# Three tiny softmax steps on ScalarE in place of VectorE, and the softmax released two sums earlier

## The chip, the cores and the metric

The kernel runs on one core of a Trainium2 chip, in FP32 throughout. The metric is the device time of one execution in microseconds; the kernel before takes 706.02 us, the median of three executions (704.77 to 706.29). The engines are named as in the profile: PE (TensorE matmul), PEld (its weight loads), DVE (VectorE), ACT (ScalarE), POOL (GpSimd) and SP (SyncE, which issues the DMAs).

## The reference

Two stages follow each other. The first is a cross attention in both directions between 512 rows x and 32 state rows per head, for 8 batches and 8 heads of width 64. The second is a feed-forward layer with an ELU over all 4352 resulting rows (per batch 512 from x and 32 from the state).

```python
B, H, S, Ns, D = (8, 8, 512, 32, 64)
scores = scale * np.matmul(x, state.transpose(0, 1, 3, 2))
scores = scores - scores.max(-1, keepdims=True)
a = np.exp(scores)
a /= a.sum(-1, keepdims=True) + 1e-09
xread = np.matmul(a, state)
scores2 = scale * np.matmul(state, x.transpose(0, 1, 3, 2))
scores2 = scores2 - scores2.max(-1, keepdims=True)
a2 = np.exp(scores2)
a2 /= a2.sum(-1, keepdims=True) + 1e-09
sread = np.matmul(a2, x)
x = np.concatenate([xread, sread], axis=2)      # then (B,H,S,D) -> (B*S, H*D)
h = x @ w_in                                    # 512 -> 2048
g = np.where(h > 0.0, h, np.exp(np.minimum(h, 0.0)) - 1.0)
out = g @ w_out                                 # 2048 -> 512
```

There are two softmaxes per batch over the same products: one over the 32 states for each row of x, and one over the 512 rows for each state.

## The kernel before, in words

**The work of a batch.** The scores of a batch lie in two PSUM banks: the 32 states of eight heads are 256 rows, in two groups g of 128, and the 512 rows of x are their columns. `softmax` (from line 751) turns them by blocks of 32 with DVE transposes into `xr`, reduces over the states (128x16 per group), subtracts on POOL, exponentiates on ACT, sums on DVE, adds eps and inverts 32 totals per partition, multiplies on POOL, and transposes into `aT`, the attention weights over the states. `softmax_rows` (from line 737) works on the same scores as they lie, over the 512 columns of each state: a maximum per row on DVE, a 128x2 step that multiplies both maxima by -scale, two exponentials on ACT that add up the totals, a 128x2 step that adds eps, and a reciprocal. The scale, eps and maxima are in the buffer `small`, 68 columns wide; batches 0 and 1 have theirs in `sec`.

The attention output is not formed for the rows of x. The weights w_in are first multiplied with the state (`make_m`, in the profile the matmuls ps<-w_half,kT), and the first phase of the FFN multiplies the result `m` with `aT` (`ffn1_chunk`, four chunks, matmuls ps<-aT,m; ELU on ACT and DVE into `g`). The second phase (`ffn2`) multiplies `g` with w_out in 128x128 passes, eight matmuls to a product. Both phases, and the split of each half, use sums of operands in a seven-product scheme in place of eight products: DVE and POOL form sums such as `s`, `sec`, `g` and sums of `aT` and `m`, PE does seven products of them, and DVE or ACT gather each product from its PSUM bank into `o` (the row o<-o,ps, called an eviction here). A product can't start before its operand sums are made, and its bank is free only after the eviction of the product that had it.

For the state rows, `move_state` turns the row weights on DVE (two transposes into `xr`) and moves them between partitions with 16 DMAs of 32 KB on SP (xr<-xr); `state_read` multiplies them with x (matmuls ps<-xe,xr), and ACT scales the result with the reciprocal totals into `kT` (ps,small). The rows of all batches go through the FFN at the end (`states`).

**The stages.** `start` and `ffn2_1` are a prologue of batches 0 and 1, in which ACT and DVE also convert the weights from memory into what the products need. Then `batch(b)` runs for b = 2 to 7, each with the first phase of batch b and `ffn2`, in which the scores, `make_m`, the softmax and the state's move of batch b+1 are also written. So the softmax of the next batch runs on DVE, ACT and POOL beside the second phase of the present one. This is called a transition here. `sum_a` and `sum_m`, written behind the softmax, are POOL's sums of `aT` and `m`.

**What sets the order.** Nothing is issued as it is written. Each operation is recorded with a cost, its operands and a `port` flag (in class `Engine`, from line 464; nearly all rows of the profile therefore carry L464), and the class `Plan` makes a list schedule of them (line 1587, `plan.order(3, 40.0)`): PE takes the ready operation that was written first, POOL keeps the written order, and DVE, ACT and SP take the ready operation whose due time is nearest, due times being counted back from PE's order. The planner lets only one operation with the flag `port` run on DVE or POOL at a time. The engines then carry out their lists in order. `plan.behind(op)` makes what is recorded within depend on op. In `ffn2` the list `late` collects such points: late[4] is the last of the sums for product 6 (`second[6].sums`), late[5] a sum o.a12 - o.s, late[6] the last of the sums for product 7 (`second[7].sums`). In `soft_next` (line 1320) the next batch's softmax, its rows, the load of x, the state's move and POOL's sums are recorded behind late[6].

Of the kernel before, what the change touches and what calls it, by code (L numbers as in the profile page):

```python
# [16 lines left out]
AF = mybir.ActivationFunctionType  # L17
ALU = mybir.AluOpType
# [16 lines left out]
def elements(ap):  # L35
    n = 1
    for k in ap.shape[1:]:
        n *= k
    return n
# [350 lines left out]
def kernel(  # L390
# [21 lines left out]
    scale = 1.0 / math.sqrt(D)  # L412
    eps = 1e-9
# [16 lines left out]
    plan = Plan(psum)  # L430
# [28 lines left out]
    def issue(engine, name, kw):  # L459
        def emit():  # L460
            named = {k: resolve(v) for k, v in kw.items()}
            if name == "memset":
                named["ap"] = named.pop("out")
            ins = getattr(engine, name)(**named)  # L464
            tc.keep_in_program_order(ins)

        return emit

    def is_ap(v):
        return isinstance(v, (View, bass.AP))  # L470

    class Engine:
# [3 lines left out]
        def __getattr__(self, name):  # L476
            def call(**kw):
                outs = [kw[k] for k in ("out", "accum_out") if k in kw]
                ins = [v for k, v in kw.items() if k not in ("out", "accum_out") and is_ap(v)]
                n = max(elements(a) for a in outs + ins) / 1000  # L480
                wide = [a for a in ins if not isinstance(a, View) and elements(a) > 4]
                port = False
                if self.key == DVE:
                    cost = 0.07 + 1.042 * n
                    alone = len(wide) == 1 and not isinstance(kw["out"], View)
                    if alone and name in ("tensor_scalar", "tensor_copy"):
                        cost, port = 0.07 + 0.53 * n, True
                    port = port or len(wide) > 1
                elif self.key == ACT:
                    cost = 0.055 + 0.84 * n  # L490
                    cost += 0.1 * sum(k in kw and is_ap(kw[k]) for k in ("scale", "bias") if k in kw)
                    cost += 0.1 * ("accum_out" in kw)
                else:
                    cost = 0.06 + (1.86 if name == "tensor_tensor" and n > 0.3 else 2.45) * n
                    port = True
                plan.add(
                    self.key, cost, issue(self.engine, name, kw), ins, outs, port,
                    name=name,
                )

            return call

    V, A, Q = Engine(DVE, nc.vector), Engine(ACT, nc.scalar), Engine(POOL, nc.gpsimd)
# [56 lines left out]
    def bc(ap, n):  # L560
        return ap[:, :, None].to_broadcast(list(ap.shape) + [n])
# [6 lines left out]
    def small(b):  # L568
        return small_2 if b > 1 else sec_1[:, 1152:1220]

    def tops(b, g):
        small_b = small(b)
        return dict(
            top=small_b[:, g : g + 1], total=small_b[:, 2 + g : 3 + g],
            top_t=small_b[:, 4 + 16 * g : 20 + 16 * g], total_t=small_b[:, 36 + 16 * g : 52 + 16 * g],
        )
# [150 lines left out]
    def soft_t(b, g):  # L727
        return (xr if b > 1 else soft)[:, g * 512 : (g + 1) * 512]

    def soft_a(b, g):  # L730
        at = xr if b > 1 else s_buf if b else sec_2
        return at[:, (b > 0) * 1024 + g * 512 :][:, :512]

    def read(b, late=False):
        return kT[:, (b - 1) % (B + 1)] if b != 1 or not late else read_1

    def softmax_rows(b):
        s = st[b, "s"]
        top, total = small(b)[:, 0:2], small(b)[:, 2:4]
        for g in range(G):  # L740
            V.reduce_max(out=tops(b, g)["top"], in_=s[g], axis=AX_X)
        V.tensor_scalar(out=top, in0=top, scalar1=-scale, scalar2=None, op0=ALU.mult)
        for g in range(G):
            A.activation(
                out=soft_a(b, g), in_=s[g], func=AF.Exp, scale=scale, bias=tops(b, g)["top"],
                accum_out=tops(b, g)["total"],
            )
        V.tensor_scalar(out=total, in0=total, scalar1=eps, scalar2=None, op0=ALU.add)
        V.reciprocal(out=total, in_=total)

    def softmax(b, to):
        s = st[b, "s"]
        total_t = small(b)[:, 36:68]

        def rows(g):
            return soft_t(b, g).rearrange("p (k n) -> p k n", n=NS)

        for g in range(G):
            V.transpose(out=soft_t(b, g), in_=s[g])
        for g in range(G):  # L760
            V.reduce_max(out=tops(b, g)["top_t"], in_=rows(g), axis=AX_X)
            (V if 0 & 1 and b > 1 or b in [] else Q).tensor_tensor(
                out=rows(g), in0=rows(g), in1=bc(tops(b, g)["top_t"], NS), op=ALU.subtract
            )
            A.activation(out=soft_t(b, g), in_=soft_t(b, g), func=AF.Exp, scale=scale)
            V.reduce_sum(out=tops(b, g)["total_t"], in_=rows(g), axis=AX_X)
        V.tensor_scalar(out=total_t, in0=total_t, scalar1=eps, scalar2=None, op0=ALU.add)
        V.reciprocal(out=total_t, in_=total_t)
        for g in range(G):
            (V if 0 & 2 and b > 1 or b in [] else Q).tensor_tensor(  # L770
                out=rows(g), in0=rows(g), in1=bc(tops(b, g)["total_t"], NS), op=ALU.mult
            )
            V.transpose(out=to[:, g * 512 : (g + 1) * 512], in_=soft_t(b, g))
# [502 lines left out]
    def ffn2(o, b):  # L1276

        c11, c12, c21, c22 = (o.part(i, j) for i in range(2) for j in range(2))
        nxt = b + 1 < B
        spare = spaces(m_sb[:, 1], 3)  # L1280
        o.sum_1()
        late = [plan.ops[-1]]
        if 0:
            second[1].sums(o.a11, spare + s_2[0][:1])
            steps = second[1].steps(c12, fresh=True)
            steps[0]()
        else:
            x1 = o.open()
            o.product(x1, o.a11, b11, True)
            A.copy(out=c12, in_=x1)  # L1290
            steps = []
        if nxt:
            first_m(b + 1, 1)
            scores(b + 1, xr, [f.view() for f in fixed])
        else:
            turn_read()
        for f in steps[1:]:
            f()
        second[2].sums(o.a12, s_2[1] + spaces(a_sb))
        late.append(plan.ops[-1])  # L1300
        for f in second[2].steps(c11, base=c12):
            f()
        late.append(plan.ops[-1])
        second[4].sums(o.a22, s_2[0] + spare[:2])
        late.append(plan.ops[-1])
        for f in second[4].steps(c21, fresh=True):
            f()
        second[6].sums(o.s, s_2[1] + spaces(a_sb))
        late.append(plan.ops[-1])
        combine(o.a12, o.a12, o.s)  # L1310
        late.append(plan.ops[-1])
        steps = second[6].steps(c12)
        second[7].sums(o.a21, s_2[0])
        late.append(plan.ops[-1])
        for f in steps:
            f()
        combine(o.s, o.s, o.a11, ALU.add)
        late.append(plan.ops[-1])

        def soft_next():  # L1320
            if nxt:
                with plan.behind(late[6]):
                    softmax(b + 1, a_sb)
                    softmax_rows(b + 1)
                    load_x(b + 1, x_halves)
                    move_state(b + 1)
                    sum_a()
                    if 1:
                        sum_m(m_to[0])
        if 1==1: soft_next()  # L1330
        V.tensor_tensor(out=c21, in0=c21, in1=c12, op=ALU.add)
        steps = second[7].steps(c22, fresh=True)
        second[5].sums(o.s, s_2[1])
        late.append(plan.ops[-1])
        if 1==2: soft_next()
        for f in steps:
            f()
        V.tensor_tensor(out=c21, in0=c21, in1=c22, op=ALU.add)
        steps = second[5].steps(c12)
        second[3].sums(o.a12, s_2[0])  # L1340
        for f in steps:
            f()
        V.tensor_tensor(out=c22, in0=c22, in1=c12, op=ALU.add)
        store(b, 1, o)
        steps = second[3].steps(c12)
        if nxt:
            make_m(b + 1, 2, 3)
            copy_m(b + 1, 1, m_to[1])
            sum_m(m_to[1])
            state_read(b + 1)  # L1350
        for f in steps:
            f()
        store(b, 0, o)
# [269 lines left out]
```

## Time and profile before

| | before |
|---|---|
| median of three executions | 706.02 us (704.77 to 706.29) |
| the profiled execution | 707.31 us |
| its span, first to last instruction | 705.5 us |
| TensorE clock granted | 0.997 |
| PE busy | 692.4 us, 98% |
| DVE busy | 577.5 us, 82% |
| ACT busy | 301.3 us, 43% |
| POOL busy | 139.4 us, 20% |
| tensor_scalar 128x2 in small on DVE, 12 | 7.5 us, mean 625 ns |
| tensor_scalar 128x32 in small on DVE, 6 | 1.0 us, mean 174 ns |
| tensor_scalar 128x2 in sec on DVE, 4 | 1.7 us, mean 431 ns |

The profile is of one execution, and its durations are compared with its own time. The 1.8 us between the profiled time and the span lie outside the instructions that it records. A line of a timeline gives start, length, engine, line of the kernel, operation, output<-inputs, shapes and how many instructions it stands for; in brackets follow the idle time before it and what ended that. In a line of groups the total busy time and the mean of one in ns stand after the bar, then the engine's idle time ahead of them. [...] Shares of busy time are averages over stages; the stages are seen in windows.

### The profile page before, as it was taken

Reading aid. Unit: us, or ns where it says so; the run is one execution under the profiler, and the core shown is the slowest. Engines: PE = TensorE matmul, PEld = TensorE weight load, DVE = VectorE, ACT = ScalarE, POOL = GpSimd, SP = SyncE. Lnnn points to the kernel's source line nnn. Section 1 sums busy time; section 2 is a strip of 40 time slices with the busy share of each in tenths; the row PEclk is TensorE's granted clock in tenths of the full one; section 3 lists DMA queues with packets and bytes.
Section 4 is the critical chain, followed back from the end, with each engine's and each line's share of the span. In section 5 each row is a group of like instructions: output and inputs, shape, how many; then the busy total and the mean of one; then the engine's idle time right before and its main releaser. Section 6 shows DMA issues by size and latency. Waiting matters only on the chain.

```text
span 705.5 us, 14564 instructions
## 1 busy us (share of the span) xinstructions
PE 692.4 (98%) x5802; PEld 591.9 (84%) x5802; DVE 577.5 (82%) x1015; ACT 301.3 (43%) x604; POOL 139.4 (20%) x161
## 2 busy tenths in 40 slices
PE   8899999999999999999999999999999999999997
PEld 7544468889988998889888988899888988899996
DVE  3989999999659895899769995989589976997650
ACT  3999982011157123831275125712383127600530
POOL 1310000042121045101630153103520173000000
PEclk9999999999999999999999999999999999999999
DMA  8677773203261406650283316440575026200300
GB/s 193 208 275 256 265 240 58 60 33 118 91 141 70 120 2 181 149 121 1 60 245 77 70 44 189 98 121 1 153 177 120 2 59 212 62 1 31 120 8 23
DMA packets 111268, 78.55 MB, mean 111 GB/s; under 512 B 89184, under 2 KB 92768, under 8 KB 111200
## 3 DMA queue, kind: packets, MB, share of 16 engines
q1 hardware_dynamic: 108988, 77.06, 38.6%
q8 instruction: 46, 0.75, 0.4%
q10 hardware_dynamic: 2212, 0.56, 0.4%
q14 instruction: 22, 0.18, 0.1%
HBM read 61.34 MB, written 13.11 MB: 106 GB/s over the span
## 4 chain that ended last, share of the span: by engine, by line
PE 82%; DVE 12%; DMA 2%; issue 2%; ACT 1%; SPq 1%; ACTq 0%; DVEq 0%
PE ps L464 82%; DVE small L464 3%; DVE o L464 3%; DVE sec L464 2%; DVE s L464 2%; DMA xe<-in_x_dram 1%; DVE g L464 1%; DMA g<-in_x_dram 1%; SPq L464 1%; DVE xr L464 0%; DVE aT L464 0%; PE ps L1581 0%; ACT sec L464 0%; ACT t_w L464 0%; ACTq L464 0%
## 5 line engine op out<-in xcount | busy, mean ns | idle before, releaser
L464 PE MATMUL ps<-aT,m 128*128 128x256 f32 (+1 forms) x568 | 148.8, 406 | 1.1 <-ACT kT L464 1.1
L464 PE MATMUL ps<-w_out,g 128*128 128x128 f32 (+1 forms) x864 | 144.5, 315 | 0.0
L464 PEld LDWEIGHTS ps<-w_out,g 128*128 128x128 f32 x864 | 126.6, 191 | 14.7 <-issue 6.2
L464 PEld LDWEIGHTS ps<-aT,m 128*128 128x128 f32 x568 | 105.1, 190 | 29.1 <-issue 13.1
L464 DVE TENSOR_TENSOR o<-o,ps 128x128 f32<-128x128 f32 (+2 forms) x239 | 66.6, 282 | 50.0 <-PE ps L464 48.5
L464 ACT COPY o<-ps 128x128 f32<-128x128 f32 (+2 forms) x70 | 23.2, 335 | 153.5 <-PE ps L464 153.5
L464 POOL TENSOR_TENSOR xr<-xr,small 128x512 f32<-128x512 f32 x24 | 26.9, 1140 | 306.9 <-PE ps L464 156.9
L464 POOL TENSOR_TENSOR m<-m 128x256 f32<-128x256 f32 x72 | 65.9, 937 | 70.8 <-ACT m L464 69.4
L464 PE MATMUL ps<-sec 128*128 128x128 f32 x560 | 74.0, 275 | 0.0
L464 PEld LDWEIGHTS ps<-sec 128*128 128x128 f32 x560 | 68.4, 192 | 0.4
L464 PE MATMUL ps<-t_w,s 128*128 128x128 f32 (+1 forms) x432 | 65.1, 300 | 3.1 <-DVE o L464 3.1
L464 PEld LDWEIGHTS ps<-t_w,s 128*128 128x128 f32 x432 | 58.4, 191 | 7.3 <-DVE o L464 4.1
L464 ACT ACTIVATE xe<-ps 128x512 f32<-128x512 f32 x96 | 55.5, 600 | 19.5 <-DVE ps L464 12.8
L464 ACT COPY m<-ps 128x512 f32<-128x512 f32 (+1 forms) x56 | 27.1, 535 | 71.8 <-PE ps L464 71.7
L464 ACT COPY sec<-ps 128x512 f32<-128x512 f32 (+1 forms) x52 | 29.8, 574 | 46.0 <-PE ps L464 45.9
L464 DVE SCALAR_TENSOR_TENSOR g<-xe,ps 128x512 f32<-128x512 f32 x66 | 43.7, 679 | 1.2 <-ACT xe L464 1.2
L464 DVE TENSOR_SCALAR xe<-xe 128x512 f32<-128x512 f32 x30 | 15.7, 527 | 31.2 <-ACT xe L464 26.1
L464 PE MATMUL ps<-aT,s 128*128 128x256 f32 x168 | 40.9, 382 | 0.0
L464 ACT ACTIVATE xe<-xe 128x512 f32<-128x512 f32 x66 | 40.0, 637 | 0.9
L464 DVE TENSOR_TENSOR ps<-sec,ps 128x512 f32<-128x512 f32 (+1 forms) x52 | 34.8, 669 | 5.7 <-PE ps L464 4.2
L464 PEld LDWEIGHTS ps<-aT,s 128*128 128x128 f32 x168 | 31.3, 190 | 6.4 <-issue 2.1
L464 PE MATMUL ps<-w_half,kT 64*32 64x256 f32 x1024 | 35.0, 382 | 0.0
(152 smaller groups left out, 1157.4 us busy)
## 6 DMA issues: line engine op xcount, KB each, us to landing
w_half<-w_in_mem SPq DMA_DIRECT2D x54, 512.0 KB
t_w<-in_moe_w_out_dram SPq DMA_DIRECT2D x8, 1024.0 KB
t_w<-in_moe_w_in_dram SPq DMA_DIRECT2D x7, 1024.0 KB
out_dram<-o SPq DMA_DIRECT2D x14, 512.0 KB
xe<-in_x_dram SPq DMA_DIRECT2D x26, 256.0 KB
o<-in_x_dram SPq DMA_DIRECT2D x80, 64.0 KB
w_in_mem<-w_half SPq DMA_DIRECT2D x8, 512.0 KB
xr<-xr SPq DMA_DIRECT2D x96, 32.0 KB
```

The lines of the kernel that those rows point to most:

```text
L464: ins = getattr(engine, name)(**named)
```

## The change

A helper `line` does a tiny step as an ACT activation Copy with an immediate scale and bias, in place of a DVE tensor_scalar with one constant. It serves three steps: the maxima times -scale (128x2), the row totals plus eps (128x2) and the state totals plus eps (128x32). Its condition b >= 0 holds for all eight batches. In the planner's costs, every tensor_scalar of DVE gets the `port` flag, also one on few elements. In `soft_next` the softmax and what is recorded with it stand behind late[4] instead of late[6].

```diff
                     if alone and name in ("tensor_scalar", "tensor_copy"):
-                        cost, port = 0.07 + 0.53 * n, True
+                        cost = 0.07 + 0.53 * n
+                    port = name == "tensor_scalar" or alone and name == "tensor_copy"
                     port = port or len(wide) > 1
...
+    def line(b, x, a, c):
+        if b >= 0:
+            A.activation(out=x, in_=x, func=AF.Copy, scale=a, bias=c)
+        elif c:
+            V.tensor_scalar(out=x, in0=x, scalar1=c, scalar2=None, op0=ALU.add)
+        else:
+            V.tensor_scalar(out=x, in0=x, scalar1=a, scalar2=None, op0=ALU.mult)
+
     def softmax_rows(b):
...
-        V.tensor_scalar(out=top, in0=top, scalar1=-scale, scalar2=None, op0=ALU.mult)
+        line(b, top, -scale, 0.0)
...
-        V.tensor_scalar(out=total, in0=total, scalar1=eps, scalar2=None, op0=ALU.add)
+        line(b, total, 1.0, eps)
...
-        V.tensor_scalar(out=total_t, in0=total_t, scalar1=eps, scalar2=None, op0=ALU.add)
+        line(b, total_t, 1.0, eps)
...
         def soft_next():
             if nxt:
-                with plan.behind(late[6]):
+                with plan.behind(late[4]):
                     softmax(b + 1, a_sb)
```

## The prediction

> **What bounds the kernel now.** I read the page's busy shares first, then windows of 10 us, the waits, and the timelines of PE, DVE and POOL in one transition.
>
> ```profile
> PE 692.4 (98%) x5802; PEld 591.9 (84%) x5802; DVE 577.5 (82%) x1015; ACT 301.3 (43%) x604; POOL 139.4 (20%) x161
> 40.00:50.00 10.00, 10.00 (x86) 4.38 (x85) 9.90 (x14) 9.40 (x19) 0.00 (x0) 1.00 0.68 232
> 330.00:340.00 10.00, 9.20 (x80) 8.82 (x79) 10.00 (x21) 2.13 (x7) 3.88 (x5) 1.00 0.01 2
> ```
>
> PE is busy 98% of the span. In the second line (columns after the length: PE, PEld, DVE, ACT, POOL) PE is full, but DVE and ACT are nearly full as well: the prologue, where batches 0 and 1 run beside the weight conversion. In the third PE misses 0.80 us while DVE is full and ACT has time. Five windows have such a hole, one per transition of batches 2 to 7; between 40 and 700 us PE is otherwise full. So only holes in PE, or work added to PE, move the time.
>
> The timeline of PE in that window, then of DVE, then of POOL:
>
> ```profile
> 334.43 1.06 PE L464 MATMUL ps<-t_w,s 128*128 128x128 f32 x8
> 335.32 1.06 PE L464 MATMUL ps<-sec 128*128 128x128 f32 x8
> 337.00 1.16 PE L464 MATMUL ps<-t_w,s 128*128 128x128 f32 x8 [0.62 <-DVE o L464]
> 338.00 1.06 PE L464 MATMUL ps<-sec 128*128 128x128 f32 x8
> 339.24 1.16 PE L464 MATMUL ps<-sec,s 128*128 128x128 f32 x8 [0.18 <-DVE o L464]
> ```
>
> ```profile
> 333.12 0.17 DVE L464 TENSOR_SCALAR small<-small 128x32 f32<-128x32 f32 x1
> 334.21 1.01 DVE L464 TENSOR_SCALAR small<-small 128x2 f32<-128x2 f32 x1
> 335.33 1.42 DVE L464 TENSOR_TENSOR sec<-g 128x512 f32<-128x512 f32 x1
> 336.67 0.28 DVE L464 TENSOR_TENSOR o<-o,ps 128x128 f32<-128x128 f32 x1
> 337.50 0.24 DVE L464 TENSOR_TENSOR o<-o,ps 128x128 f32<-128x128 f32 x1
> 337.67 0.72 DVE L464 TENSOR_SCALAR small<-small 128x2 f32<-128x2 f32 x1
> ```
>
> ```profile
> 333.89 2.31 POOL L464 TENSOR_TENSOR xr<-xr,small 128x512 f32<-128x512 f32 x2 [7.69 <-DVE small L464]
> 337.65 0.72 POOL L464 TENSOR_TENSOR aT<-aT 128x256 f32<-128x256 f32 x1 [1.45 <-DVE aT L464]
> ```
>
> Groups of eight matmuls start 0.89 us apart (335.32 - 334.43). From 335.32 to 337.00 it is 1.68: PE lost 0.79, because the eviction that frees its PSUM bank (336.67, which ends at 336.95) was queued on DVE behind the 1.42 us sum and the 1.01 us tiny step. 338.00 to 339.24 is 0.35 too long, behind the 0.72 us tiny step. The first loss is in all five transitions (0.78 each), the second in two (0.345): 5 x 0.78 + 2 x 0.345 = 4.6 us, all that a change in the steady state can win by filling holes. The view of waits says much the same, less the start-up after each hole, and shows where the softmax idles:
>
> ```profile
> PE ps L464 <- DVE o L464: 3.7, 8, 0.6
> ...
> ACT xr L464 <- POOL xr L464: 21.6, 11, 3.7
> ACT xr L464 <- DVE small L464: 19.0, 6, 3.8
> ```
>
> [...] the 2-column step at 334.21 lasts 1.01 us inside POOL's 333.89 to 336.20, and the 32-column one ahead of it 0.17. [...] the trace holds a single table load of 1.28 us, so I cost table switches at nothing.
>
> ```profile
> L464 DVE TENSOR_SCALAR small<-small 128x2 f32<-128x2 f32 x12 | 7.5, 625 | 0.0
> L464 ACT ACTIVATION_READ_ACCUMULATOR xr<-ps,small 128x1 f32 x12 | 2.4, 196 | 0.0
> L464 ACT ACTIVATE kT<-ps,small 128x64 f32<-128x64 f32 x12 | 3.2, 329 | 0.0
> ```
>
> **The change, part by part.** (1) 24 tiny steps leave DVE for ACT: three per softmax, eight softmaxes. In a transition DVE is relieved of 0.17 + 1.01 + 0.72 = 1.9 us. Not all is a gain: part of it was waiting for POOL, and the next two-input sum inherits the wait. ACT gains 3 x 0.2 = 0.6 us where it is busy 2.13 of 10; that alone costs nothing.
>
> (2) The softmax may start after the sums of product 6, no longer after product 7's. In the new written order its reduces stand about 6 us earlier on DVE (I follow the order with the pitches of the old trace: evictions 0.20, sums of 512 0.60, transposes 0.63, reduces 0.60). In the transition shown the row reduces then end near 322, ACT's scale near 322.2, exp rows near 323.8, the eps steps at 324.2 and 327.3, the reciprocals at 328.3. POOL multiplies from 328.4 to 331.6, the transposes into aT follow at 330.8 to 332.8, and POOL's sums of aT run from 332 to 340. The old places were 333.89 and 337.65. What is late next: these POOL steps now meet DVE's two-input sums for products 5 and 3 (s 128x1024, sec and s 128x512). By that reckoning the operand s of a t_w,s product, read at PE's 338.33, is ready at 338.49 (about 0.16 us of stall); three other places have 0.2 to 0.4 of slack. I take 0.25 per transition, with bounds of 0 and 0.8: 5 x 0.25 = 1.25 stays of the 4.6.
>
> (3) The changed port flag alters nothing by itself: with the old flag the written order of the changed kernel comes out the same, since the only steps it would mark anew are now on ACT. But new costs and an earlier softmax make the planner order everything anew. On PE the scores of the moved state (the xe,xr run) now stand between runs of full passes in all six transitions, where they used to adjoin the kT run. In the old trace the starts at the borders of such an isolated run are 93 and 101 ns too far apart, 0.2 us together: 6 x 0.2 = +1.2 us (bounds 0 and 1.5). Nothing hides that: PE is full.
>
> (4) The state's move is 16 DMAs on SP, about 0.63 us from issue to issue, each landing about 1.9 us later. The first now goes at about 334.5, so the last starts near 344 and lands near 346, with the load of the next w_half beside them; the xe,xr run starts near 347.6. Slack 1.2 us: no cost. If the first were over 1.2 us later, PE would lose the excess in each transition.
>
> (5) In the prologue six of the steps join an ACT that is 9.40 to 10.00 of 10 busy: 6 x 0.2 = 1.2 us more ACT time, and as much less on DVE (431 ns each there). Queued behind them are ACT's evictions and exponentials, for which PE waits with slack of 0.06 to 1.1 us near 48 and 65 us. PE enters its full stretch about 0.16 us later in the new order; I take +0.5 (bounds -0.5 and +1.5).
>
> Sum: -4.6 + 1.25 + 1.2 + 0 + 0.5 = -1.65 us. The profiled execution took 707.31 (span 705.5), so it would take 705.7 (span 703.9). The median shown, 706.02, is 1.3 lower; the same difference gives **704.4**. About 0.2%, 1.4 us, is what a measurement of this kernel can tell from no change: faster is below 704.6, slower above 707.4.
>
> **Rivals.** *All of it comes* (0.24): no stall left, the prologue neutral: -4.6 + 1.2 = -3.4, 702.6. For: the hole hangs on tiny steps that vanish from DVE. Against: POOL keeps as much work and DVE as many two-input sums[...].
>
> *The stall only moves* (0.18): [...] PE stalls 0.78 per transition at another place: -4.6 + 3.9 + 1.2 + 0.5 = +1.0, 707.0. For: the new order has four two-input sums inside 332 to 340. Against: those have 0.2 us of slack where the eviction in the old order had less than none.
>
> *Slower by the prologue* (0.12): ACT works in written order. A tiny step that waits for a DVE reduce blocks the exponentials behind it; with six of them and DVE itself 9.90 of 10 busy, a wait of 0.7 us each, about one reduce, is 4.2 us that both engines lack, and PE follows. With the steady state's -4.6 + 1.25 + 1.2 that is +2.05, and with the switching of ACT to late work about +2.5: 708.5. It decides from 3.5 us of prologue loss up (-4.6 + 1.25 + 1.2 + 3.5 = +1.35). For: the windows above. Against: only two softmaxes are there.
>
> **How the numbers follow.** The likeliest case has 0.46 (its own range 703.2 to 705.6, from the bounds of 3 and 5 in part); it gives 0.265 faster, 0.17 same, 0.025 slower. The full gain gives 0.24 faster. The moved stall splits 0.01, 0.08, 0.09, the prologue 0, 0.02, 0.10. Sums: faster 0.52, same 0.27, slower 0.21. The range 702.2 to 707.6 leaves out about a third of the full gain at its low end, and most of the prologue case.
>
> **What would show it.** Right: no TENSOR_SCALAR of 2 columns in `small` on DVE, twelve ACTIVATE of about 0.2 us on ACT; in the windows of the five transitions PE over 9.6; the wait of PE for DVE o below 1.5 us in all. Step 2: POOL's xr,small steps within 1 us after its reciprocal, near 5 us earlier relative to the transition. Step 3: the isolated xe,xr run with 0.1 us at each border. Step 4 wrong: PE waits for a DMA xr<-xr. Step 5: the start of batch 2's first phase compared in both traces; more than 1.5 us late means the prologue rival. The prediction fails if PE's holes stay at 0.8 under another name, or if the new order opens holes that the old did not have.

## The result, and the profile after

The changed kernel takes 703.02 us, the median of 20 executions (702.0 to 706.83), against 705.94 us of 20 executions of the kernel before. The ratio is 0.9966, 95% interval 0.9958 to 0.9975: faster by 0.34%, 1.8 to 3.0 us. The forecast was 704.4. The profiled execution took 704.65 us with a span of 702.9 (before 707.31 and 705.5).

First the busy shares and the windows of the transition that the prediction followed (columns after the length: PE, PEld, DVE, ACT, POOL):

```profile
PE 692.8 (99%) x5794; PEld 591.0 (84%) x5794; DVE 563.8 (80%) x991; ACT 303.9 (43%) x628; POOL 144.2 (21%) x161
320.00:330.00 10.00, 10.00 (x92) 10.00 (x92) 9.79 (x23) 3.44 (x11) 3.12 (x4) 1.00 0.00 0
330.00:340.00 10.00, 10.00 (x113) 9.34 (x112) 8.37 (x16) 1.87 (x5) 9.75 (x10) 1.00 0.10 25
```

PE has no hole: 10.00 of 10 where it had 9.20. Every window of 10 us from 50 to 690 us reads 10.00 now. DVE, which was full, has 1.6 us to spare in the second of them. POOL is busy 9.75 us of the ten.

The same transition in the timelines, PE first, then DVE, POOL and ACT. Times of this trace stand 0.69 us later than those of before at the scores ahead of it (308.12 against 307.43).

```profile
334.24 1.06 PE L464 MATMUL ps<-w_out,g 128*128 128x128 f32 x8
335.13 1.06 PE L464 MATMUL ps<-t_w,s 128*128 128x128 f32 x8
336.12 1.09 PE L464 MATMUL ps<-w_half,kT 64*32 64x256 f32 x32
...
339.03 1.06 PE L464 MATMUL ps<-t_w,s 128*128 128x128 f32 x8
```

```profile
324.78 1.23 DVE L464 TENSOR_TENSOR s<-s,g 128x1024 f32<-128x1024 f32 x1
...
328.50 0.38 DVE L464 RECIPROCAL small<-small 128x32 f32<-128x32 f32 x2
...
329.29 1.77 DVE L464 TENSOR_TENSOR s<-s,g 128x1024 f32<-128x1024 f32 x1
...
337.04 1.21 DVE L464 TENSOR_TENSOR s<-s 128x512 f32<-128x512 f32 x1
339.23 0.29 DVE L464 TENSOR_TENSOR o<-o,ps 128x128 f32<-128x128 f32 x1 [0.98 <-PE ps L464]
```

```profile
320.62 2.05 POOL L464 TENSOR_TENSOR xr<-xr,small 128x512 f32<-128x512 f32 x2 [29.25 <-PE ps L464]
328.93 3.04 POOL L464 TENSOR_TENSOR xr<-xr,small 128x512 f32<-128x512 f32 x2 [6.25 <-DVE small L464]
331.96 1.15 POOL L464 TENSOR_TENSOR aT<-aT 128x256 f32<-128x256 f32 x1
```

```profile
323.25 0.19 ACT L464 ACTIVATE small<-small 128x2 f32<-128x2 f32 x1
...
324.95 0.22 ACT L464 ACTIVATE small<-small 128x2 f32<-128x2 f32 x1
327.63 0.23 ACT L464 ACTIVATE small<-small 128x32 f32<-128x32 f32 x1 [2.45 <-DVE small L464]
```

Three things are to be seen. The tiny steps cost ACT about 0.2 us each, before POOL's multiplies begin at 328.93. POOL's two multiplies start 20.81 us after the scores, where they started 26.46 us after them. And the last operand for the product at 339.03 is ready at 338.25 (337.04 + 1.21), 0.78 us early; DVE then waits for PE, not PE for DVE. DVE and POOL still lengthen each other's work: DVE's 128x1024 sum takes 1.77 us beside POOL's multiplies, and 1.23 at 324.78; POOL's pair takes 3.04 us, and 2.05 at 320.62. But in this transition PE no longer waits behind it.

The groups of the tiny steps:

```profile
L464 ACT ACTIVATE small<-small 128x2 f32<-128x2 f32 x12 | 2.4, 203 | 3.1 <-DVE small L464 3.1
L464 ACT ACTIVATE small<-small 128x32 f32<-128x32 f32 x6 | 1.4, 229 | 15.6 <-DVE small L464 15.6
```

**A ruler for the steady part.** PE is full, so what a change does in one stage can be read from landmarks of PE's work. The row of matmuls ps<-xr,kT that each transition leads up to (the next batch's scores; the seventh and last time, the state's rows turned) stands at the same amount of PE work in all kernels here, wherever else the orders differ: from one such row to the next every trace has the same matmuls, by number and shape (776, then 688 four times, then 656). Two of them in the kernel before, then in the changed one:

```profile
231.03 1.06 PE L464 MATMUL ps<-xr,kT 64*32 64x512 f32 x16
307.43 1.06 PE L464 MATMUL ps<-xr,kT 64*32 64x512 f32 x16
```

```profile
232.33 1.06 PE L464 MATMUL ps<-xr,kT 64*32 64x512 f32 x16
308.12 1.06 PE L464 MATMUL ps<-xr,kT 64*32 64x512 f32 x16
```

Between these, 76.40 us became 75.79. In the two transitions that had the second hole it was 76.86 and 76.90, and became 75.80 and 75.79. I call the start of the first such row, near 138 us, "the first scores", and the time from there to the start of the last matmul "the steady part". It is 562.37 and 562.40 us in two profiles of the kernel before, and 558.99 and 558.96 in two of the changed one: it repeats within 0.03, far better than the whole time, and is 3.4 us shorter. The other kernels below have one profile each. Ahead of the first row stand 832 matmuls of the work in every kernel, beside fill matmuls (`fill`) that the planner puts into PE's idle time in the first 36 us: 98 before, 90 in the changed kernel.

### The profile page after: what moved, and what is told of

Read it like the earlier page. It is cut to its first block, busy times and chain, and to the rows that moved or that the text cites. A ratio compares the mean times of both kernels' runs of the same rounds, so it can differ in the third digit from the quotient of the medians.

```text
span 702.9 us, 14562 instructions
## 1 busy us (share of the span) xinstructions
PE 692.8 (99%) x5794; PEld 591.0 (84%) x5794; DVE 563.8 (80%) x991; ACT 303.9 (43%) x628; POOL 144.2 (21%) x161
## 4 chain that ended last, share of the span: by engine, by line
PE 94%; ACT 2%; DMA 2%; DVE 1%; SPq 1%; issue 0%; ACTq 0%; DVEq 0%
PE ps L464 93%; DMA g<-in_x_dram 1%; DMA xe<-in_x_dram 1%; SPq L464 1%; DVE w_half L464 1%; ACT sec L464 1%; ACT w_half L464 0%; ACT t_w L464 0%; PE ps L1590 0%; ACT m L464 0%; DVE sec L464 0%; DVE t_w L464 0%; ACTq L464 0%; DVE g L464 0%; ACT g L464 0%
## 5 line engine op out<-in xcount | busy, mean ns | idle before, releaser
L464 DVE TENSOR_TENSOR o<-o,ps 128x128 f32<-128x128 f32 (+2 forms) x239 | 68.8, 289 | 66.9 <-PE ps L464 66.2
L464 POOL TENSOR_TENSOR xr<-xr,small 128x512 f32<-128x512 f32 x24 | 30.9, 1306 | 290.5 <-PE ps L464 147.1
L464 POOL TENSOR_TENSOR m<-m 128x256 f32<-128x256 f32 x72 | 63.6, 907 | 52.0 <-ACT m L464 50.6
L464 ACT COPY ps<-ps 128x512 f32<-128x512 f32 (+1 forms) x28 | 15.1, 541 | 61.2 <-PE ps L464 61.2
```

## Experiments

All ratios are to the kernel before on the same chip, with their 95% intervals. Kernels that are told as "in the old order" or "in the new order" have each engine's other instructions in exactly that order; only the tiny steps are issued to another engine or in another form.

| kernel | median, us | ratio | first scores, us | steady part, us |
|---|---|---|---|---|
| before (two profiles) | 705.94 | 1 | 138.04, 136.66 | 562.37, 562.40 |
| changed (two profiles) | 703.02 | 0.9966 | 138.76, 138.18 | 558.99, 558.96 |
| old order, tiny steps on ACT | 701.43 | 0.9941 | 137.38 | 557.15 |
| new order, tiny steps on DVE | 704.16 | 0.9971 | 137.29 | 559.62 |
| on ACT with late[6], ordered anew | 702.76 | 0.9962 | 136.51 | 558.70 |
| late[4] alone, ordered anew | 704.04 | 0.9972 | 137.44 | 560.15 |
| old order, only the scale step on ACT | 701.90 | 0.9940 | 136.69 | 557.42 |
| old order, on DVE by single columns | 700.92 | 0.9931 | 136.35 | 557.13 |
| late[4] and single columns | 701.71 | 0.9937 | 136.79 | 558.28 |
| port flag alone | 705.70 | 1.0003 | 141.52 | 557.80 |
| changed, with batches 0 and 1 on DVE | 705.89 | 1.0009 | 142.66 | 559.08 |
| port flag for batches 2 to 7 alone | 701.97 | 0.9938 | 138.88 | 557.97 |

### The engine and the order, taken apart

**Old order, the tiny steps on ACT.** The planner counts the step as before, and only what is issued is replaced:

```diff
+    def on_act(x, a, c):
+        plan.ops[-1].emit = issue(
+            nc.scalar, "activation", dict(out=x, in_=x, func=AF.Copy, scale=a, bias=c)
+        )
...
         V.tensor_scalar(out=top, in0=top, scalar1=-scale, scalar2=None, op0=ALU.mult)
+        on_act(top, -scale, 0.0)
```

(and likewise for the two eps steps)

> The old written order of every engine is kept and only the 24 tiny steps are carried out by ACT instead of DVE, at their old places. Theory A (the holes of 0.78 and 0.345 us are the time that tiny steps spend on DVE waiting for POOL's multiplies): the holes shrink to below 0.2 us each, no isolated matmul run is added, the prologue stays: 702.0 us, ratio 0.994 to 0.996. Theory B (the new order is what helps[...]): holes of 0.5 us and more stay, 704.5 us, ratio 0.997 to 0.999.

Measured: 701.43 us, ratio 0.9941 (0.9929 to 0.9953). No hole is left in the transitions. DVE and POOL at the place of the first hole:

```profile
332.73 1.34 DVE L464 TENSOR_TENSOR sec<-g 128x512 f32<-128x512 f32 x1
333.99 0.27 DVE L464 TENSOR_TENSOR o<-o,ps 128x128 f32<-128x128 f32 x1
```

```profile
332.15 2.82 POOL L464 TENSOR_TENSOR xr<-xr,small 128x512 f32<-128x512 f32 x2 [7.54 <-DVE small L464]
```

The two-input sum still waits for POOL (1.34 us, where it had 1.42). The wait of the tiny step isn't handed on to it; POOL's pair takes 2.82 us in place of 2.31, so POOL bears a part. On ACT the eps step took 0.21 us at 333.20, in the midst of POOL's pair. The single instructions of the two traces show how. Before, DVE waited twice in a row: the tiny step ended at 335.22, just behind POOL's first multiply (335.19), and the sum at 336.75, 0.55 us behind the second (336.20). In this run the sum ends 0.55 us behind the first multiply (334.07 and 333.52), and POOL's second lasts 1.49 us instead of 1.04, until 334.97: now POOL waits for DVE. So each time DVE had to wait out one of POOL's multiplies, and without the tiny step it does so once ahead of the eviction instead of twice. Theory A held: in the old order, the engine alone empties the holes.

**New order, the tiny steps on DVE.** In `line`, an engine object that plans as ACT and issues to DVE:

```diff
+    AV = Engine(ACT, nc.vector)
...
-            A.activation(out=x, in_=x, func=AF.Copy, scale=a, bias=c)
-        elif c:
-            V.tensor_scalar(out=x, in0=x, scalar1=c, scalar2=None, op0=ALU.add)
-        else:
-            V.tensor_scalar(out=x, in0=x, scalar1=a, scalar2=None, op0=ALU.mult)
+            if c:
+                AV.tensor_scalar(out=x, in0=x, scalar1=c, scalar2=None, op0=ALU.add)
+            else:
+                AV.tensor_scalar(out=x, in0=x, scalar1=a, scalar2=None, op0=ALU.mult)
```

> The new written order of every engine is kept and only the 24 tiny steps are carried out by DVE, at the places in time that the planner gave them on ACT. Theory B (the order is what helps: the tiny steps no longer fall into POOL's multiplies, and DVE has over 3 us of idle time in a transition): as fast as the changed kernel, 703.0 to 703.4 us, ratio 0.996 to 0.9965, tiny steps of below 0.2 us. Theory A (the engine is what helps): 704.5 to 706 us, tiny steps of 0.6 us and more, holes in PE again.

Measured: 704.16 us, ratio 0.9971 (0.9964 to 0.9978), beside 0.9966 for the changed kernel. The steps:

```profile
L464 DVE TENSOR_SCALAR small<-small 128x2 f32<-128x2 f32 x12 | 2.8, 229 | 0.0
```

229 ns in place of 625, a little above the 0.2 us expected. The time lies between the ranges of both theories. But no hole is left in the transitions, as Theory B had it, and in the new order the engine is worth only some 0.6 us of the steady part (559.62 - 558.99). So I had put the two theories as exclusive, and they aren't: either the engine or the order empties the holes, and the second of them has little left to win.

**Each edit alone, ordered anew by the planner.** First the change with late[6] kept, then late[4] in the kernel before.

```diff
-                with plan.behind(late[4]):
+                with plan.behind(late[6]):
```

> The change without the earlier release (late[6] kept), all ordered anew by the planner. Theory A: nearly the whole gain, 702.5 to 703.5 us. Theory B: the softmax comes as late as before and POOL's multiplies still meet the evictions: 704.5 to 706 us.

Measured: 702.76 us, ratio 0.9962 (0.9949 to 0.9974), within Theory A's numbers.

```diff
-                with plan.behind(late[6]):
+                with plan.behind(late[4]):
```

> The earlier release alone (late[4]), the tiny steps on DVE with the old costs and flags, all ordered anew. Theory A: tiny steps wait for POOL as before, 705 to 706 us. Theory B: the holes go with the order, 703 to 704 us.

Measured: 704.04 us, ratio 0.9972 (0.9961 to 0.9982): Theory B's 703 to 704 but for 0.04 us, and not Theory A's. Holes of 0.53 us are left in three transitions. Each edit alone, ordered anew, has most of the gain or all of it. They don't add.

### The wait for POOL itself

**Single columns.** If its form is what makes a step of two columns wait for POOL, the step must become short on the same engine at the same place once the form is another. That a single column is such a form, no trace had shown so far. So each 128x2 step was issued as two of 128x1, on DVE, in the order of the kernel before:

```diff
+    def by_column(x, c, op):
+        emits = [
+            issue(
+                nc.vector, "tensor_scalar",
+                dict(out=x[:, g : g + 1], in0=x[:, g : g + 1], scalar1=c, scalar2=None, op0=op),
+            )
+            for g in range(G)
+        ]
...
         V.tensor_scalar(out=top, in0=top, scalar1=-scale, scalar2=None, op0=ALU.mult)
+        by_column(top, -scale, ALU.mult)
```

(and likewise for the eps step of the row totals)

> The kernel before, in its order and with all steps on DVE; only each 128x2 step is issued as two steps of one column (128x1). Theory P [...]: each column takes below 0.15 us, also inside POOL's multiplies, the holes go to below 0.2 us each and the time is that of the old order with the steps on ACT, 701.4 to 702.3 us, ratio 0.994 to 0.9955. Theory L (any tensor_scalar waits, or the position alone delays the evictions): the columns take 0.5 us and more, holes as before or larger, 706 us and more.

Measured: 700.92 us, ratio 0.9931 (0.9917 to 0.9945), 0.5 us below the range given. This is faster than the kernel before and the changed one. The group, then two of the steps on DVE, then POOL at the time:

```profile
L464 DVE TENSOR_SCALAR small<-small 128x1 f32<-128x1 f32 x24 | 2.3, 137 | 0.0
```

```profile
331.62 0.20 DVE L464 TENSOR_SCALAR small<-small 128x1 f32<-128x1 f32 x2
...
334.07 0.19 DVE L464 TENSOR_SCALAR small<-small 128x1 f32<-128x1 f32 x2
```

```profile
331.30 2.76 POOL L464 TENSOR_TENSOR xr<-xr,small 128x512 f32<-128x512 f32 x2 [7.69 <-DVE small L464]
334.05 0.73 POOL L464 TENSOR_TENSOR aT<-aT 128x256 f32<-128x256 f32 x1
```

Two columns pass in 0.20 us in the midst of POOL's multiply, and in 0.19 beside its sum of aT, where the one step of two columns took 1.01 and 0.72. So it hangs on the step's form whether it has to wait for POOL here. Theory P, as far as it puts the wait down to the form, held so far; by what means the form does it, no run here shows. Steady part (557.13 against 557.15) and, within the intervals, ratio are those of the old order with the steps on ACT: neither DVE's work on these steps nor ACT's was the matter, but the wait.

**Only the scale step on ACT,** in the old order (`on_act` for `top` alone):

> The kernel before, in its order; only the steps that multiply the maxima by -scale are carried out by ACT, at their old places (the step of 1.01 us in the transition shown). Theory A: the holes of 0.78 us, five times, go, and the two of 0.345 us behind the eps step stay: 705.9 - 4.4 + 0 = about 702.0 us, ratio 0.994 to 0.996. If the eps step or the next two-input sum inherits the wait instead: holes of 0.4 us and more stay in all five transitions, 703.5 to 705 us.

Measured: 701.90 us, ratio 0.9940 (0.9926 to 0.9954), steady part 557.42. The holes of 0.78 us go, as expected. Of the two of 0.345 us one of 0.22 is left, in one transition, where I had expected both to stay: of the five eps steps on DVE in these transitions that one still waits for POOL (0.73 us), and the other four take 0.14 to 0.15. Before, two of the five took 0.73, and in its second profile two others, so it wasn't the same ones in both executions. Moving one of the three steps gives nearly the whole gain.

**The earlier release with single columns** (late[4] in the kernel before, and `by_column` for both 128x2 steps):

> The earlier release alone (late[4], old costs and flags, the order of the kernel with the earlier release alone), with each 128x2 step on DVE issued as two one-column steps[...]. Theory P: what holes the earlier release alone had left go too; against the one-column kernel in the old order it pays 0.25 us for an isolated xe,xr run in each of five transitions, about 1.3 us: 702.2 us, ratio 0.994 to 0.9955. If the earlier release has a gain of its own[...]: 701 us or less.

Measured: 701.71 us, ratio 0.9937 (0.9924 to 0.9950), 0.5 us below the forecast and just below the range given for the ratio. The steady part is 558.28, 1.15 us longer than with single columns in the old order, near the 1.3 expected. So the earlier release has no gain of its own once no tiny step waits for POOL; by the steady part it costs (the two ratios are too near each other to tell).

### The planner's flag, and the prologue

**The port flag alone** (the changed kernel with the condition b >= 99, so that the tiny steps stay on DVE, and late[6]):

> The port flag alone: tiny steps on DVE as 128x2, release behind late[6], but the planner now [...] keeps them out of POOL's steps. If telling the planner is enough: tiny steps of below 0.3 us, no holes of 0.5 us, and 0.25 us for each isolated xe,xr run: 702.5 to 703.5 us, ratio 0.995 to 0.9965. If not, since the planner keeps its times only roughly: tiny steps of 0.5 us and more, 705 us and more.

Measured: 705.70 us, ratio 1.0003 (0.9985 to 1.0020). The time lies in the second range, but not for the reason given there. The steady part is 557.80 us, 4.6 less than before, although the 128x2 steps still take 455 ns on average, more than the 0.3 us expected; but the first scores come at 141.52. The flag empties the transitions and loses it all in the prologue. PE, then ACT, at that place:

```profile
64.06 1.53 PE L464 MATMUL ps<-w_half,kT 64*32 64x256 f32 x48
68.64 1.48 PE L464 MATMUL ps<-w_half,kT 64*32 64x256 f32 x32 [3.06 <-ACT m L464]
```

```profile
65.16 1.13 ACT L464 ACTIVATE w_out<-t_w 128x1024 f32<-128x1024 f32 x1 [2.88 <-DMA t_w<-in_moe_w_out_dram]
66.20 0.58 ACT L464 ACTIVATE sec<-ps 128x512 f32<-128x512 f32 x1
66.68 1.14 ACT L464 ACTIVATE t_w<-t_w 128x1024 f32<-128x1024 uint32 x1
67.70 0.62 ACT L464 ACTIVATE sec<-sec 128x512 f32<-128x512 f32 x1
68.22 0.64 ACT L464 COPY m<-ps 128x256 f32<-128x256 f32 x2
```

In this order a weight conversion stands on ACT ahead of the copies into m, and waits 2.88 us for its DMA; the copies wait behind it, and PE waits 3.06 us for them. That is the place and the kind of loss that the prologue rival named, head of ACT's queue, with another releaser: a DMA, not a DVE reduce.

**The changed kernel with the six steps of batches 0 and 1 on DVE** (the condition b >= 2):

> The changed kernel with the six tiny steps of batches 0 and 1 left on DVE (18 on ACT), ordered anew. If the six steps on ACT cost the prologue 0.5 us, as the prediction had it: 702.5 us, ratio 0.995 to 0.9963. If they cost nothing there: that of the changed kernel, 0.996 to 0.997.

Measured: 705.89 us, ratio 1.0009 (0.9998 to 1.0020), outside both ranges. The steady part, 559.08, is that of the changed kernel; the first scores come at 142.66, and ACT waits 2.09 us for the same DMA ahead of the same copies. These two kernels have in common that the six steps of the prologue are on DVE with the new flag, and their matmuls up to the first scores come in the same order, which no other kernel here has.

**The flag for batches 2 to 7 alone** (in the kernel before, after each of the three steps):

```diff
+        plan.ops[-1].port = plan.ops[-1].port or b > 1
```

> The port flag for the tiny steps of batches 2 to 7 alone; those of batches 0 and 1 keep the old planning, and PE's order in the prologue is that of the kernel before. If the flag's loss lay only in the prologue (the hole of 3.4 us at 65 us, where ACT stands before a weight DMA ahead of the copies into m), and the flag by itself empties the holes of the transitions: 4.6 us less than before, 701.4 us, ratio 0.9925 to 0.995. If the transitions gain nothing from it: 704.5 to 706 us.

Measured: 701.97 us, ratio 0.9938 (0.9924 to 0.9951), within the range given and 0.6 us above the 701.4. The flag's loss lay in the prologue alone, and its gain in the transitions is nearly whole (steady part 557.97). Here too the tiny steps still wait. DVE, then POOL, in one transition:

```profile
334.41 0.82 DVE L464 TENSOR_SCALAR small<-small 128x2 f32<-128x2 f32 x1
335.24 0.71 DVE L464 STREAM_TRANSPOSE aT<-xr 128x512 f32<-128x512 f32 x1
335.88 0.25 DVE L464 TENSOR_TENSOR o<-o,ps 128x128 f32<-128x128 f32 x1
```

```profile
333.90 2.31 POOL L464 TENSOR_TENSOR xr<-xr,small 128x512 f32<-128x512 f32 x2 [7.69 <-DVE small L464]
```

The scale step takes 0.82 us inside POOL's multiplies, as it does in all five transitions, and PE has no hole. A transpose, 0.71 us long beside POOL's second multiply (0.705 on average in this run), follows it in place of the two-input sum, which had taken 1.42. (In the profile before, the seven transposes into aT that start beside an instruction of POOL take 698 ns on average, the other five 699; evictions into o, 279 beside POOL and 278 apart from it.) The eviction comes at 335.88, where before it came at 336.67 with the step in nearly the same place. So the tiny step's wait alone stays hidden; in the kernel before, the sum's wait came on top of it ahead of the same eviction.

### Two repeats

> The changed kernel once more, beside the kernels that take it apart: ratio 0.9958 to 0.9975 as found. If its prologue has no cost of its own, a profile at full clock has the start of its second product (kT run near 46 us) at the same time as the kernel before in its profile at full clock, within 0.3 us; if the prologue costs what the first two profiles show, 0.6 us or more later.

> The kernel before once more, for a profile at full clock in the first 40 us: the same five holes of 0.78 us and two of about 0.345 us; span about 704 us, since the first profile was taken at a granted clock of 0.87 between 20 and 30 us.

Measured: the changed kernel at 703.39 us, ratio 0.9963 (0.9950 to 0.9975); the kernel before at 706.0, with a span of 704.1. The kernel before had its five holes of 0.78 us and two of 0.345 again, the latter in two other transitions. The profile of the changed kernel was again one with a granted clock of 0.89 between 20 and 30 us (0.84 the first time), so this pair doesn't compare both prologues at full clock; other runs do, under step 5 below.

## Why the prediction was right, and where its sum was off

The sign, the cause and the range held; 703.02 lies between the likeliest case (704.4, own range from 703.2) and the case in which all of it comes (702.6). By its steps:

1. **The tiny steps.** Right. They moved from 625 to 203 ns (128x2) and are 229 ns at 128x32. The 0.2 us of the prediction was my estimate; in the profile before, the nearest rows on ACT are 196 ns at 128x1 and 329 at 128x64. No table load came with the steps: the trace holds one, of 1.28 us, as before.

2. **The holes.** This is the term that was mis-sized, twice. The pool was put at 4.6 us and is 5.2: between the scores of two batches 76.40 us fell to 75.52 in the old order without waits (304.84 - 229.32), so the hole of 0.78 was worth 0.88. After each hole the next group takes 0.10 us more, as the prediction's own fence showed (337.00 to 338.00 is 1.00, not 0.89), and there were seven holes: 4.6 + 0.7. And I left 1.25 us of holes in the five transitions, where none is left. I had reckoned an operand ready 0.16 us late that came 0.78 us early. That fits with waits that I had put down to DVE and that POOL bore (its pair took 3.04 us in place of 2.31), for which PE doesn't wait; how much of the 0.9 us this makes, no run separates. So the term reads -5.2 where I had -4.6 + 1.25 = -3.35. What the prediction named as the cause is shown by the old order with the steps on ACT and by single columns. That the same gain could be had from the order alone I hadn't separated.

3. **The new order's own cost.** Forecast +1.2 for six isolated xe,xr runs. In the five transitions from batch 2 on, the changed kernel takes 378.03 us from the second to the seventh row of scores, single columns in the old order 376.74: +1.29, 0.26 each. Its isolated run, between full passes:

```profile
346.95 1.05 PE L464 MATMUL ps<-sec 128*128 128x128 f32 x8
347.94 1.10 PE L464 MATMUL ps<-xe,xr 128*32 128x64 f32 x64
348.97 1.16 PE L464 MATMUL ps<-w_out,g 128*128 128x128 f32 x8
349.96 0.28 PE L464 MATMUL ps<-sec 128*128 128x128 f32 x1
```

Both neighbours take 0.99 us instead of 0.89, 0.10 at each border, as forecast. The other 0.06 or 0.07 in each transition are short delays among the matmuls ps<-aT,m (0.20 us against 0.13), whose cause I haven't followed. The first transition, into batch 2, costs +0.58 (93.57 between the first two rows of scores, before 92.99), of which I had 0.2; it goes with the order, for with the steps back on DVE in the new order it is 93.56. There DVE's evictions are late near 168 and 169 us beside POOL's sums of m: 0.10 and 0.14 us of holes with 0.10 of restart each, a small form of the rival in which the stall only moves. Sum: +1.87, where I had +1.2.

4. **The state's move.** Right. The first DMA goes at 334.68, the last, issued at 344.17, lands at 345.99, the xe,xr run starts at 347.94: 1.95 us to spare where I had 1.2, and no wait of PE for xr<-xr.

5. **The prologue.** Forecast +0.5; no such cost is seen. The first scores came 0.72 us later in the first pair of profiles, both at a lowered clock. But in the eight profiles with the old order of the prologue they come anywhere between 136.35 and 138.88, and in the four with the new order between 136.51 and 138.76. At full clock it is 136.35 to 137.44 in six with the old order, 136.51 and 137.29 in two with the new. And from the prologue's one row ps<-g,xr (55.65 us before, 56.31 in the changed kernel) to the first scores it is 82.40 us in all eight, and 82.45 to 82.47 in the four. A cost below the scatter of the first 56 us isn't excluded.

The steady part sums to -5.2 + 1.87 = -3.3 (measured 3.4), and with the prologue's 0 to 0.7 to between -3.4 and -2.6; the medians differ by 2.92, and the ratio gives 2.4 with 1.8 to 3.0. The forecast was -1.65. That it came so near is in part luck: the gain from the holes and the cost of the new order were both put too low, and the two errors have opposite signs. The rival in which the prologue makes the kernel slower didn't come here, but two kernels with part of the change taken back did just that, at 3 to 4 us and at the place in question: so it was a real rival. The other rival, the stall that only moves, came as 0.44 us in one transition.

Of the change, then, only one part was needed. The tiny steps on ACT in the old order are 1.6 us faster than the change as made (701.43 against 703.02; 1.8 us in the steady part), since they need no new order.

## What to carry to other kernels

When the same short instruction takes times that differ several times over (here 0.15 to 1.01 us for the step of two columns), look for what it waits on, and for what stands behind it: here one wait was hidden, and two in a row ahead of an eviction that PE needed were not. A change of form at the same place can be worth as much as a change of engine. Where a planner writes the order, take the order and the edit apart by keeping one and changing the other; here the gain of the edit was 5.2 us and the new order gave back 1.9. And a cost flag is felt everywhere it applies: the flag that emptied five transitions lost about as much in a stage that it wasn't meant for.

## What was not expected of the hardware

A hole in PE cost more than its length: the group after it took about 0.10 us more, in all seven cases of the first profile before (1.00 us instead of 0.89 behind the five long ones).

A tensor_scalar of one column (128x1) on DVE took 137 ns on average and 175 at most, also beside POOL; the same step on two columns took 0.15 us at 142.33, where it met no instruction of POOL, 1.01 behind a multiply, and 625 ns on average. In the transition shown, DVE and POOL took turns by whole instructions: in the old order with the steps on ACT, DVE's sum waited out POOL's first multiply (1.34 us), and then POOL's second took 1.49 us instead of 1.04.

The start varies by 2.5 us, nearly as much as the change is worth. In four of twelve profiles (those without the hole at 65 us) the granted clock between 20 and 30 us was 0.83 to 0.89, and the first scores came at 138.0 to 138.9 us; in the eight at 1.00 they came at 136.4 to 137.4. That is why the whole time of one execution could not settle the prologue's term, and the steady part could settle the others. It isn't the number of fill matmuls that decides: two of the four had 98 and two had 90, and so had profiles at full clock. What lowers the clock in some executions stays open.
